# Long convolution with a routed expert step: spreading the loads over each pass, folding in the joint part in single steps, and giving every second set of folds to VectorE

## The chip, the cores and the metric

The kernel runs on one core of a Trainium2 chip. The metric is the device time of one execution in microseconds (us). The engines are TensorE (PE in the profile; its weight loads are PEld), VectorE (DVE), ScalarE (ACT), GpSimd (POOL) and SyncE (SP), which here only issues DMA transfers. Each engine works through its own instructions in the order in which they were written. SyncE does the same with its transfers: a transfer whose condition isn't met yet holds up those written after it.

## The reference

`x` has 8 batches of 6336 positions and 128 features, `h` is a filter of 6336 positions for each feature. The first part is a causal convolution along the positions, by FFT. The second part scores every position of a batch, takes the 128 best, puts them through a two-layer expert and adds the gated result.

```python
L = 2 * S
Xf = np.fft.rfft(x, n=L, axis=1)
Hf = np.fft.rfft(h, n=L, axis=0)
y = np.fft.irfft(Xf * Hf[None], n=L, axis=1)[:, :S, :]
...
scores = np.einsum('bsd,d->bs', y, w_gate)
for b in range(B):
    top_idx = np.argpartition(-scores[b], 128)[:128]
    xe = y[b, top_idx]
    ye = np.maximum(xe @ w1, 0.0) @ w2
    g = 1.0 / (1.0 + np.exp(-scores[b, top_idx]))
    out[b, top_idx] = xe + g[:, None] * ye
```

## The kernel before

The transform is done as matrix products. The work is cut into 8 **passes** (`i` from 0 to 7), each for two batches and half of the features. A pass's data comes in 8 **blocks** `g` of 512 KB (`load_x`, L142). Global block numbers run on: 0 to 7 are the filter, 8 to 15 pass 0, 16 to 23 pass 1, and so on; the text counts a block within its set of 8.

These steps turn up in the profile under their lines:

- `fold` makes of a block its difference and its sum, two elementwise operations of 128 x 512 (L155 into `odd`, which lies in `two` or in `slots`; L156 in place). Both are on GpSimd, except at the start.
- `stage_a` multiplies the folded block with `fa` on TensorE (L169); ScalarE copies the result to `ys` (L183).
- `stage_b` works on 13 **chunks** of 8 wavenumbers. TensorE multiplies with a table that is loaded for each chunk (`load_w`, L197; matmuls at L211), VectorE multiplies with the filter's spectrum (`load_h`, L203; four operations at L220), GpSimd combines (L231). When a chunk is done, the table and the spectrum of the third chunk on are loaded.
- `weigh` adds one of 64 columns of `ys` into the scores, one VectorE operation each (L308).
- `stage_c` multiplies with `wc` (L329), ScalarE copies to `zs` (L335). `stage_d` multiplies with the tables `at` (`load_at`, L348; matmuls at L359), ScalarE copies (L367), and the result is stored (L369).
- A **route** (`scores`, `pick`, `gather`, `expert`) handles the two batches of a pair of passes: scores and the search for the 128 best run on VectorE and TensorE in odd passes, the gathers (L502) and the two experts (L544, L556) in the even pass behind it, or at the end. Its steps are put between the others by `aside`.

All order is written out by hand. The program starts with the filter and pass 0 through `stage_a` (to about 50 us), then comes the **joint part**, `stage_b_first`, where the filter and pass 0 go through stage B together (L265, L281, L284; 13 steps `ci`, to 95 us). Then the passes follow. A pass has 33 **items**: 17 of stage C and 16 of stage D of this pass. Into the items, stages A and B of the *next* pass are put by `plan`: one block of stage A per item in items 0 to 7 (pass 0 takes two at item 0), then two chunks of stage B at each of seven items, which are 8, 10, 12, 14, 16, 17, 19 in even passes and 9, 13, 17, 20, 23, 26, 29 in odd ones. In even passes, the weighing of this pass goes with stage C, and that of the next pass with the items above 19. Odd passes weigh nothing.

Block `g + 2` is folded in the item of block `g`; the first two blocks of the next set are folded at block 7. Blocks have five buffers (`RX`), so block `g + 5` is loaded when stage A of `g` has been through TensorE. Three chunk tables (`RW`) and three of the spectrum (`RH`) are held, and six `at` tiles (`RA`).

At a pass's border the loads stand together: at its end three of the spectrum and six of `at`, at its beginning three tables of 512 KB. The constants of the route and the expert's weights (1 MB) are loaded at item 12 of pass 0. In the joint part, the first six `at` and the first three of the spectrum are loaded from step 7 on, and blocks 0 and 1 of the next set are folded on VectorE in the last two steps.

Of the kernel before, what the change touches and what calls it, by code (L numbers as in the profile page):

```python
# [12 lines left out]
ALU = mybir.AluOpType  # L13
# [7 lines left out]
NU = 8  # L21
# [8 lines left out]
RX, RW, RH, RA = 5, 3, 3, 6  # L30
kchunks = [(k, min(KC, N1 - k)) for k in range(0, N1, KC)]
NC = len(kchunks)
# [3 lines left out]
def conv_moe(ctx, tc, x, h, wg_d, w1, w2, fa_d, wb_d, wc_d, at_d, wgl_d, tri_d, cst_d, tw_d, fb_d, *out):  # L36
# [61 lines left out]
    pos = cp.tile([N1, 2, 2, 66], BF16, name="pos")  # L98
    acc = cp.tile([128, 2, 2, 2, N1], F32, name="acc")

    def load_constants(later):
        if not later:
            sp.dma_start(out=wc, in_=wc_d)
            sp.dma_start(out=wgl, in_=wgl_d)
            return
        sp.dma_start(out=tri, in_=tri_d)
        sp.dma_start(out=cst, in_=cst_d)
        sp.dma_start(out=wg, in_=wg_d.rearrange("(o d) -> o d", o=1).broadcast_to([128, D]))
        sp.dma_start(out=tw, in_=tw_d)
        sp.dma_start(out=fb, in_=fb_d)  # L110
        sp.dma_start(out=w1s, in_=w1)
        sp.dma_start(out=w2s, in_=w2.rearrange("(c p) d -> p c d", p=128))

    def make_constants():
        v.tensor_copy(out=upper16, in_=upper)
# [10 lines left out]
    raw, odd = {}, {}  # L126
# [14 lines left out]
        src = h if i < 0 else x[i]  # L141
        sp.dma_start(out=raw[g], in_=src[:, n].rearrange("p (s d n) -> p s d n", s=2, d=8))  # L142

    def fold(g, eng):
        if g >= 8 * (NU + 1):
            return
        a = raw[g]
        if g < 16:
            o = low(1, 512, g % 7)
        elif g % 8 % 3 < 2:  # L150
            o = two[:, g % 8 % 3]
        else:
            o = low((g // 8 - 1) % 2, 512, 6)
        odd[g] = o.rearrange("p (d n) -> p d n", d=8)
        eng.tensor_tensor(out=odd[g], in0=a[:, 1], in1=a[:, 0], op=ALU.subtract)  # L155
        eng.tensor_tensor(out=a[:, 0], in0=a[:, 0], in1=a[:, 1], op=ALU.add)  # L156

    def stage_a(g, r, dve=()):
        a, o = raw.pop(g), odd.pop(g)
# [39 lines left out]
    def load_h(u, ci):  # L199
        if ci < NC:  # L200
            k0, kn = kchunks[ci]
            hts[u, ci] = tp.tile([128, 2, KC, 32], F32, tag="h", name="ht", bufs=RH)
            sp.dma_start(out=hts[u, ci][:, :, 0:kn], in_=hd[:, ci, u, :, 0:kn])  # L203
# [106 lines left out]
    def stage_c(i, weighing=True):  # L310
        r = i % 2
        y = ys[r].rearrange("p (j c) k t -> p j c k t", c=2)
        z = zs[r].rearrange("p (n g j) m t -> p n g j m t", g=2, j=2)
        banks = [None, None]
        n = 0
        for s in range(66):
            while weighing and n < min(64, 8 * s // 5 + 5):
                weigh(i, n)
                n += 1
            cols = [s, s - 2]  # L320
            for g in range(2):
                if 0 <= cols[g] < 64 and cols[g] % 4 == 0:
                    banks[g] = psa()
            for ri in range(2):
                for g in range(2):
                    c = cols[g]
                    if 0 <= c < 64:
                        rows = slice(g * 64, g * 64 + 64)
                        pe.matmul(banks[g][0:N1, c % 4 * 128:c % 4 * 128 + 128], y[rows, c // 2, ri, :, c % 2],  # L329
                                  wc[rows, ri], start=(ri == 0), stop=(ri == 1))  # L330
            on_pe(0.49)
            for g in range(2):
                c = cols[g]
                if 0 <= c < 64 and c % 4 == 3:
                    act.copy(out=z[:, c // 4, g].rearrange("p j m t -> p j t m"),  # L335
                             in_=banks[g][0:N1].rearrange("p (j t m) -> p j t m", j=2, t=2))
            if i == NU - 1 or (i % 2 and s in (46, 62)):
                aside()
            if s % 4 == 3 or s == 65:
                yield  # L340
# [3 lines left out]
    def load_at(n):  # L344
        if n < 17:
            k = min(2, NT - 2 * n)
            ats[n] = tp.tile([N1, 2, 2, N1], F32, tag="at", name="at", bufs=RA)
            sp.dma_start(out=ats[n][:, 0:k], in_=at_d[:, 2 * n:2 * n + k])  # L348
# [254 lines left out]
    with tc.manual_schedule():  # L603
# [16 lines left out]
        for ci in range(NC):  # L620
            stage_b_first(ci)
            if ci == 3:
                load_constants(False)
            if ci in (4, 5, 6, 9, 10):
                load_x(16 + (4, 5, 6, 9, 10).index(ci))
            if ci >= NC - 2:
                fold(18 + ci - NC, v)
            if 7 <= ci:
                load_at(ci - 7)
            if ci >= NC - RH:  # L630
                load_h(1, ci - NC + RH)

        for i in range(NU):
            phase[0] = i
            if i < NU - 1:
                for ci in range(RW):
                    load_w((i + 1) % 2, ci)
            cs, ds = stage_c(i, i % 2 == 0), stage_d(i)
            g0 = 16 + 8 * i
            plan = {}  # L640
            if i < NU - 1:
                for n in range(8):
                    plan.setdefault(max(0, n - (i == 0)), []).append(("a", n))
                for n, at_item in enumerate((8, 10, 12, 14, 16, 17, 19) if i % 2 == 0 else (9, 13, 17, 20, 23, 26, 29)):
                    plan[at_item] = [("b", k) for k in range(2 * n, min(NC, 2 * n + 2))]
            early = 0
            calm[0] = 0.3 if i < NU - 1 else 0.0
            for item in range(33):
                place[0] = item
                strand = cs if item < 17 else ds  # L650
                if i == 0 and item == 12:
                    load_constants(True)
                if i == 0 and item == 20:
                    make_constants()
                if item in plan:
                    aside()
                    for kind, k in plan[item]:
                        if kind == "a":
                            g = g0 + k
                            if g % 8 < 6:  # L660
                                fold(g + 2, pool)
                            elif g % 8 == 7:
                                fold(g + 1, pool)
                            stage_a(g, (i + 1) % 2)
                            load_x(g + RX)
                            if g % 8 == 7:
                                fold(g + 2, pool)
                        else:
                            stage_b(i + 1, k)
                if i % 2 == 0 and item > 19:  # L670
                    for _ in range(5):
                        if early < 64:
                            weigh(i + 1, early)
                            early += 1
                next(strand, None)
            for st in (cs, ds):
                for _ in st:
                    pass
            if i < NU - 2:
                for ci in range(RH):  # L680
                    load_h(i % 2, ci)
            if i < NU - 1:
                for n in range(RA):
                    load_at(n)
        phase[0] = NU
        idle(7)
        for _ in routes:
# [135 lines left out]
```

## Time and profile before

| | |
|---|---|
| time, median of 3 runs | 954.77 us (952.27 to 965.12) |
| the profiled execution | 949.83 us, span 948.1 us |
| TensorE busy | 889.5 us, 94% of the span |
| VectorE busy | 663.7 us, 70% |
| GpSimd busy | 473.1 us, 50% |
| ScalarE busy | 386.0 us, 41% |
| HBM traffic | 135.38 MB read, 32.96 MB written, 178 GB/s over the span |
| mean granted clock of TensorE | 0.968 |

A row of a chain of work gives start, length and what ran: an engine with the line of the kernel, or a transfer. A row of waits says who waited for whom: microseconds in total, times, the longest. In a row of a timeline, the bracket at the end is the idle time of that engine just before. A row of stretches gives for each engine its busy time and, in brackets, its number of instructions, then the granted clock, the DMA share and the rate. A matmul of 32-bit floats shows as two instructions.

### The profile page before, as it was taken

What the parts mean: (1) busy time and instruction counts of PE and PEld (TensorE: products, weight loads), DVE (VectorE), ACT (ScalarE), POOL (GpSimd) and SP (SyncE); (2) the same over time, 40 slices, a digit from 0 to 9 for tenths busy, and PEclk for the clock granted to TensorE, in tenths of its full rate; (3) what the DMA queues carried; (4) which work ended last, traced back from release to release, by engine and by line L of the source; (5) the groups of instructions that cost most, each with busy time, mean ns of one, the idle gap of its engine ahead of it and who ended that gap; (6) DMA issues with size and microseconds to landing.
All of it is one profiled execution on the core that took longest, in us unless ns stands there. A gap on an engine that the chain in (4) does not pass through costs nothing.

```text
span 948.1 us, 37606 instructions
## 1 busy us (share of the span) xinstructions
PE 889.5 (94%) x16548; PEld 793.2 (84%) x16548; DVE 663.7 (70%) x1488; ACT 386.0 (41%) x612; POOL 473.1 (50%) x376
## 2 busy tenths in 40 slices
PE   5799898999999699999999969999999989999996
PEld 5799797889987689878988769978998779978875
DVE  6467996776688937784788928793779847696631
ACT  4523552248412543237421633236621543234531
POOL 0068875526455686526554586714646475630002
PEclk8899799999999989999999989999999979999999
DMA  9557757467474746457465836457456614543051
GB/s 358 205 194 269 245 156 240 148 185 260 142 238 142 265 138 181 133 160 266 136 218 181 275 97 195 149 154 272 139 166 236 211 59 156 163 146 108 7 179 35
DMA packets 74096, 170.79 MB, mean 180 GB/s; under 512 B 10478, under 2 KB 26828, under 8 KB 73932
## 3 DMA queue, kind: packets, MB, share of 16 engines
q1 hardware_dynamic: 72908, 167.33, 54.0%
q8 instruction: 130, 2.13, 0.9%
q0 software_dynamic: 1024, 1.05, 0.5%
q14 instruction: 34, 0.28, 0.1%
HBM read 135.38 MB, written 32.96 MB: 178 GB/s over the span
## 4 chain that ended last, share of the span: by engine, by line
PE 85%; DMA 5%; POOL 5%; DVE 2%; issue 2%; SPq 0%; ACT 0%; POOLq 0%; ACTq 0%; DVEq 0%
PE pa L359 24%; PE pa L329 24%; PE pb L211 17%; PE pb L169 10%; PE pb L265 3%; DMA xr<-in_x 3%; POOL slots L155 3%; PE pa L265 2%; PE m L544 1%; PE m L556 1%; PE pa L169 1%; POOL xr L156 1%; DMA slots<-tab_wb 1%; PE m L381 1%; DVE acc L308 1%
## 5 line engine op out<-in xcount | busy, mean ns | idle before, releaser
L231 POOL TENSOR_TENSOR slots<-slots,tx 128x512 f32<-128x512 f32 (+1 forms) x182 | 231.2, 1301 | 161.3 <-DVE tx L220 161.2
L329 PE MATMUL pa<-wc,slots 64*99 64x128 f32 x4096 | 268.2, 279 | 2.9 <-issue 2.9
L329 PEld LDWEIGHTS pa<-wc,slots 64*99 64x99 f32 x4096 | 243.9, 170 | 16.5 <-issue 4.8
L335 ACT COPY slots<-pa 99x512 f32<-99x512 f32 x256 | 163.5, 639 | 193.2 <-PE pa L329 185.9
L359 PE MATMUL pa<-slots,at 99*99 99x256 f32 (+1 forms) x1056 | 232.9, 374 | 0.7 <-ACT slots L335 0.7
L308 DVE SCALAR_TENSOR_TENSOR acc<-slots,wgl,acc 128x198 f32<-128x198 f32 x496 | 208.0, 493 | 2.6 <-POOL slots L231 2.6
L359 PEld LDWEIGHTS pa<-slots,at 99*99 99x99 f32 x1056 | 164.4, 163 | 51.8 <-ACT slots L335 0.9
L220 DVE TENSOR_TENSOR slots<-pb,ht 128x512 f32<-128x512 f32 (+1 forms) x182 | 119.5, 657 | 105.6 <-issue 59.4
L211 PEld LDWEIGHTS pb<-slots 128*64 128x64 f32 x5544 | 169.3, 137 | 13.3 <-issue 8.4
L211 PE MATMUL pb<-slots 128*64 128x64 f32 x5544 | 176.5, 223 | 4.0 <-DMA slots<-tab_wb 3.7
L367 ACT COPY yt<-pa 99x512 f32<-99x512 f32 x128 | 75.0, 586 | 225.1 <-PE pa L359 219.7
L183 ACT COPY slots<-pb 128x792 f32<-128x792 f32 x130 | 110.7, 901 | 72.9 <-PE pb L169 72.7
L169 PE MATMUL pb<-fa,xr 50*64 50x99 f32 x1840 | 99.7, 258 | 21.9 <-POOL xr L156 18.8
L220 DVE TENSOR_TENSOR tx<-pb,ht 128x512 f32<-128x512 f32 (+1 forms) x182 | 118.8, 653 | 0.0
L169 PEld LDWEIGHTS pb<-fa,xr 50*64 50x64 f32 x1840 | 87.1, 140 | 34.7 <-POOL xr L156 19.5
L155 POOL TENSOR_TENSOR slots<-xr 128x512 f32<-128x512 f32 x13 | 36.6, 2812 | 106.4 <-PE pa L359 56.7
L169 PE MATMUL pb<-fa,two 50*64 50x99 f32 x1344 | 71.1, 255 | 4.4 <-issue 4.4
L156 POOL TENSOR_TENSOR xr<-xr 128x512 f32<-128x512 f32 x53 | 72.7, 1372 | 4.2
L284 POOL TENSOR_TENSOR slots<-slots,tx 128x256 f32<-128x256 f32 (+1 forms) x50 | 37.9, 782 | 61.5 <-DVE tx L281 59.9
L155 POOL TENSOR_TENSOR two<-xr 128x512 f32<-128x512 f32 x40 | 60.8, 1520 | 10.9 <-PE pb L169 10.5
L502 POOL DMA_INDIRECT xe<-out,iu x16 | 15.6, 978 | 100.3 <-DMA out<-yt 88.3
L169 PE MATMUL pb<-fa,slots 50*64 50x99 f32 x1040 | 51.4, 290 | 12.1 <-DVE slots L156 6.7
(151 smaller groups left out, 702.1 us busy)
## 6 DMA issues: line engine op xcount, KB each, us to landing
slots<-tab_wb SPq DMA_DIRECT2D x86, 512.0 KB
xr<-in_x SPq DMA_DIRECT2D x59, 512.0 KB
out<-yt SPq DMA_DIRECT2D x128, 198.0 KB
ht<-hd SPq DMA_DIRECT2D x84, 256.0 KB
at<-tab_at SPq DMA_DIRECT2D x128, 153.1 KB
hd<-slots SPq DMA_DIRECT2D x12, 512.0 KB
slots<-in_h SPq DMA_DIRECT2D x8, 512.0 KB
xr<-tab_wb SPq DMA_DIRECT2D x8, 512.0 KB
```

The costliest lines, as they stand in the source:

```text
L155: eng.tensor_tensor(out=odd[g], in0=a[:, 1], in1=a[:, 0], op=ALU.subtract)
L156: eng.tensor_tensor(out=a[:, 0], in0=a[:, 0], in1=a[:, 1], op=ALU.add)
L169: pe.matmul(bank[c * 64:c * 64 + 64, d * N1:(d + 1) * N1], src, fa[rows, c], start=True, stop=True)
L183: act.copy(out=to, in_=src)
L211: pe.matmul(banks[c][g * 64:g * 64 + 64, j * 64:j * 64 + 64], wt[:, j, c * 64:c * 64 + 64], y[:, g, :, k0 + j], start=True, stop=True)
L220: v.tensor_tensor(out=dst, in0=banks[c][:, 0:kn * 64].rearrange("p (k b j t) -> p k b j t", k=kn, b=2, t=2), in1=ht[t].rearrange("p k (j t ...
L231: pool.tensor_tensor(out=d3, in0=d3, in1=tx.rearrange("p k (j t) -> p k j t", t=2), op=ALU.add if c else ALU.subtract)
L308: v.scalar_tensor_tensor(out=dst, in0=col, scalar=w, in1=dst, op0=ALU.mult, op1=ALU.add)
L329: pe.matmul(banks[g][0:N1, c % 4 * 128:c % 4 * 128 + 128], y[rows, c // 2, ri, :, c % 2], wc[rows, ri], start=(ri == 0), stop=(ri == 1))
L335: act.copy(out=z[:, c // 4, g].rearrange("p j m t -> p j t m"), in_=banks[g][0:N1].rearrange("p (j t m) -> p j t m", j=2, t=2))
L359: pe.matmul(pt[0:N1, o:o + w * 128], ats[tau // 2][:, tau % 2, c], z[:, c, q:q + w], start=(c == 0), stop=(c == 1))
L367: act.copy(out=yt.rearrange("p b q d -> p q b d"), in_=pt[0:N1].rearrange("p (q b d) -> p q b d", q=4, b=2))
```

## The change

1. `load_constants` has three parts. `wc` and `wgl` stay in the joint part; the route's five small constants come at item 16 of pass 0 instead of item 12 (what is made of them at item 24 instead of 20); the expert's two weights come at item 20 of pass 1.
2. The three tables and three spectra of the next pass are loaded one by one in items 1 to 6 of each pass, in turn, and the six `at` in items 9 to 14 (2 to 7 in the last pass). They leave the joint part, the pass's beginning and its end.
3. Blocks 0 and 1 of the set behind the joint part are folded in steps 8 to 11 of it, one of the four operations per step, still on VectorE.
4. In even passes the folds of blocks 2 to 7 are on VectorE instead of GpSimd. Blocks 0 and 1, and all of the odd passes, stay on GpSimd.
5. Weighings of stage C are spread more thinly: five per item instead of six or seven.

```diff
-    def load_constants(later):
-        if not later:
+    def load_constants(part):
+        if part == 0:
             sp.dma_start(out=wc, in_=wc_d)
             sp.dma_start(out=wgl, in_=wgl_d)
+        if part == 2:
+            sp.dma_start(out=w1s, in_=w1)
+            sp.dma_start(out=w2s, in_=w2.rearrange("(c p) d -> p c d", p=128))
+        if part != 1:
             return
...
-    def fold(g, eng):
+    def fold(g, eng, part=0):
...
-        eng.tensor_tensor(out=odd[g], in0=a[:, 1], in1=a[:, 0], op=ALU.subtract)
-        eng.tensor_tensor(out=a[:, 0], in0=a[:, 0], in1=a[:, 1], op=ALU.add)
+        if part < 2:
+            eng.tensor_tensor(out=odd[g], in0=a[:, 1], in1=a[:, 0], op=ALU.subtract)
+        if part != 1:
+            eng.tensor_tensor(out=a[:, 0], in0=a[:, 0], in1=a[:, 1], op=ALU.add)
...
-            while weighing and n < min(64, 8 * s // 5 + 5):
+            while weighing and n < min(64, 5 * s // 4 + 5):
...
             if ci in (4, 5, 6, 9, 10):
                 load_x(16 + (4, 5, 6, 9, 10).index(ci))
-            if ci >= NC - 2:
-                fold(18 + ci - NC, v)
-            if 7 <= ci:
-                load_at(ci - 7)
-            if ci >= NC - RH:
-                load_h(1, ci - NC + RH)
+            if 8 <= ci < 12:
+                fold(12 + ci // 2, v, 1 + ci % 2)
 
         for i in range(NU):
             phase[0] = i
-            if i < NU - 1:
-                for ci in range(RW):
-                    load_w((i + 1) % 2, ci)
...
+            at_first = 9 if i < NU - 1 else 2
...
-                if i == 0 and item == 12:
-                    load_constants(True)
-                if i == 0 and item == 20:
+                if i == 0 and item == 16:
+                    load_constants(1)
+                if i == 0 and item == 24:
                     make_constants()
+                if i == 1 and item == 20:
+                    load_constants(2)
+                if i < NU - 1 and 1 <= item < 7:
+                    (load_h if item % 2 == 0 else load_w)((i + 1) % 2, (item - 1) // 2)
+                if 0 <= item - at_first < RA:
+                    load_at(item - at_first)
...
                             if g % 8 < 6:
-                                fold(g + 2, pool)
+                                fold(g + 2, pool if i % 2 else v)
...
-            if i < NU - 2:
-                for ci in range(RH):
-                    load_h(i % 2, ci)
-            if i < NU - 1:
-                for n in range(RA):
-                    load_at(n)
```

More of the change, by code (lines that the diff above doesn't have):

```diff
@@ L110, in load_constants @@
         sp.dma_start(out=fb, in_=fb_d)
-        sp.dma_start(out=w1s, in_=w1)
-        sp.dma_start(out=w2s, in_=w2.rearrange("(c p) d -> p c d", p=128))
     def make_constants():
@@ L622, in conv_moe @@
             if ci == 3:
-                load_constants(False)
+                load_constants(0)
             if ci in (4, 5, 6, 9, 10):
                 load_x(16 + (4, 5, 6, 9, 10).index(ci))
-            if ci >= NC - 2:
-                fold(18 + ci - NC, v)
-            if 7 <= ci:
-                load_at(ci - 7)
-            if ci >= NC - RH:
-                load_h(1, ci - NC + RH)
+            if 8 <= ci < 12:
+                fold(12 + ci // 2, v, 1 + ci % 2)
         for i in range(NU):
             phase[0] = i
-            if i < NU - 1:
-                for ci in range(RW):
-                    load_w((i + 1) % 2, ci)
             cs, ds = stage_c(i, i % 2 == 0), stage_d(i)
```

## The prediction

> **What bounds the kernel now.** I read the page's head, then the table of TensorE's waits, then the busy time by pass, then the chain around each gap, then the queues that the chain names.
>
> ```profile
> span 948.1 us, 37606 instructions
> PE 889.5 (94%) x16548; PEld 793.2 (84%) x16548; DVE 663.7 (70%) x1488; ACT 386.0 (41%) x612; POOL 473.1 (50%) x376
> PE pb L169 <- POOL xr L156: 18.8, 3, 7.7
> ```
>
> TensorE is busy for 94% and no other engine is near it, so time can only come from TensorE's gaps and from what follows them. The third line is its longest wait: three times it stood for a fold on GpSimd (L156 is the fold's addition). Busy time by stretch, in the order PE, PEld, DVE, ACT, POOL, granted clock, DMA share and GB/s, puts these in passes. The stretches are the joint part, then passes 0, 1, 2, 4 and 6:
>
> ```profile
> 50.00:95.00 45.00, 45.00 (x774) 44.75 (x770) 33.75 (x95) 15.34 (x32) 34.34 (x46) 0.99 0.73 245
> 95.00:205.60 110.60, 103.56 (x1951) 92.10 (x1951) 94.81 (x201) 43.62 (x64) 65.11 (x46) 0.94 0.60 193
> 205.60:306.90 101.30, 101.18 (x1993) 88.91 (x1995) 71.41 (x160) 43.32 (x64) 56.53 (x43) 1.00 0.61 198
> 306.90:423.00 116.10, 106.84 (x2016) 95.47 (x2017) 86.51 (x188) 46.65 (x76) 66.57 (x50) 0.97 0.55 175
> ...
> 524.00:642.00 118.00, 108.93 (x2027) 96.81 (x2027) 87.86 (x194) 47.06 (x78) 68.62 (x51) 0.97 0.55 174
> 743.00:862.00 119.00, 112.62 (x2023) 100.16 (x2022) 87.72 (x194) 46.82 (x77) 63.52 (x46) 0.94 0.47 150
> ```
>
> Pass 1 takes 101 us with hardly a gap and the clock at 1.00. Passes 2, 4 and 6 take 116 to 119, pass 0 takes 110.6. What should they take? The blocks of the chain at full clock give it:
>
> ```profile
> 339.19 1.52 PE pb L169 x60
> 340.71 1.93 PE pa L329 x32
> 346.09 3.92 PE pb L211 x128
> 284.57 4.43 PE pa L359 x20
> ...
> 934.26 2.68 PE pa L544 x24
> 939.62 1.80 PE pa L556 x16
> ```
>
> A pass holds 8 blocks of L169 (12.2 us), 16 of L329 (30.9), 99 x 8 matmuls of L211 (24.3) and 33 x 4 of L359 (29.2): 96.6 us. Two experts take 934.26 to 941.42, 7.2 us, and passes 2, 4 and 6 hold two each: 104 us. So pass 0 loses 14.0 us, the other even passes 12 to 15 each.
>
> The chain of pass 2, and SyncE's queue ahead of it:
>
> ```profile
> 316.45 9.27 DMA xr<-in_x
> 325.85 6.62 POOL slots L155
> 333.86 2.92 PE pb L169 x64
> ...
> 564.57 3.92 PE pb L211 x128
> ...
> 784.85 3.93 PE pb L211 x118
> ```
> ```profile
> 308.29 1.29 SPq L203 DMA_DIRECT2D ht<-hd  x3
> ...
> 313.91 2.43 SPq L197 DMA_DIRECT2D slots<-tab_wb  x3
> 316.45 28.18 SPq L142 DMA_DIRECT2D xr<-in_x  x8
> ```
> ```profile
> 324.00:326.00 2.00, 0.72 (x12) 0.73 (x14) 2.00 (x8) 0.00 (x0) 0.15 (x1) 1.00 1.02 414
> ```
>
> Stage A's first block ended near 308.4 (306.9 + 1.52) and freed the buffer of block 5, but its load was issued only at 316.45: twelve loads stood ahead, three of the spectrum, six of `at` (the line left out) and three tables, 3.2 MB by the sizes in the code, 8 us at the 414 GB/s of a full stretch. It landed 9.27 us later. Then the fold, on GpSimd, lasted 6.62 us. With L169 and L329 alternating, an item lasts 3.45 us; eight items from 306.9 end at 334.5, but the first L211 stands at 346.09. Loss: 11.6 us, of which 1.4 is the slow block after the gap (2.92 against 1.52). The same reckoning from 524.0 and 743.0 to the first L211 of passes 4 and 6 (564.57, 784.85) gives 13.0 and 14.3. Sum 38.9 us.
>
> Pass 0 loses at two places. At the joint part's end:
>
> ```profile
> 97.65 0.27 PE L169 MATMUL pb<-fa,xr 50*64 50x99 f32 x1 [2.65 <-issue]
> 96.41 1.14 DVE L156 TENSOR_TENSOR xr<-xr 128x512 f32<-128x512 f32 x1
> 98.27 0.34 DVE L281 TENSOR_TENSOR tx<-pb,slots 128x192 f32<-128x192 f32 x1
> 103.44 3.66 PE pa L329 x24
> 107.10 2.47 PE pb L169 x64
> 100.00:104.00 4.00, 3.82 (x77) 3.31 (x71) 4.00 (x4) 2.25 (x3) 3.92 (x3) 0.50 1.05 376
> ```
>
> The row calls the 2.65 us "issue", but L169 starts as the fold's L156 ends (97.55). The fold also holds back the last multiplications, which free the PSUM pair for the block's second half. Two blocks of L169 should take 3.04 us from 95.0; L329 begins at 103.44, so 5.4 us are lost, and at clock 0.50 the next blocks lose (3.66 - 1.45) + (2.47 - 1.52) = 3.2 more. Later the constants:
>
> ```profile
> PE pb L211 <- DMA slots<-tab_wb: 3.7, 1, 3.7
> 152.27 0.43 SPq L112 DMA_DIRECT2D w2s<-in_w  x1
> 152.80 7.18 DMA slots<-tab_wb
> 160.11 3.59 PE pb L211 x64
> ```
>
> Seven loads of constants, 1.5 MB, went ahead of a table that TensorE was waiting for; the last of them is the first SyncE row here. That is 3.7 us of gap and 3.59 - 1.96 = 1.6 us of slow block, 5.3.
>
> **The change part by part.** Prices of VectorE first. Rows: weighings with GpSimd held out (325.8 to 331.4), weighings beside folds on GpSimd (308.2 to 315.8), ten weighings in passes 2 and 0 beside L231, a fold operation on VectorE alone (min/median/max), one step of L220.
>
> ```profile
> L308 DVE SCALAR_TENSOR_TENSOR acc<-slots,wgl,acc 128x198 f32<-128x198 f32 x17 | 5.8, 411 | 0.0
> L308 DVE SCALAR_TENSOR_TENSOR acc<-slots,wgl,acc 128x198 f32<-128x198 f32 x7 | 9.8, 1468 | 0.0
> 353.02 4.98 DVE L308 SCALAR_TENSOR_TENSOR acc<-slots,wgl,acc 128x198 f32<-128x198 f32 x10
> 137.57 6.09 DVE L308 SCALAR_TENSOR_TENSOR acc<-slots,wgl,acc 128x198 f32<-128x198 f32 x10
> L155 DVE TENSOR_TENSOR slots<-slots x11: 683/687/694, 5.2 to 29.5; 128x512 f32<-128x512 f32 x11
> 144.26 0.60 DVE tx L220
> ```
>
> A weighing costs 0.34 us alone, 1.4 beside GpSimd's folds, 0.50 to 0.61 beside L231. While VectorE ran its weighings without a break, GpSimd's fold lasted until they ended: that is the 6.62.
>
> The Trainium skill (SBUF - State Buffer, "SBUF: two separate sides") calls the port pair of VectorE and GpSimd an exclusive lock, held for one instruction, with the other engine fully blocked. The rows agree on blocking, and go further: 17 instructions passed while GpSimd waited. By this rule the single folds in the joint part meet L284 there; the terms below stay as they are.
>
> *Loads.* Tables (L197), spectrum (L203) and `at` (L348) leave the pass's border: one load per item, w at items 1, 3, 5, h at 2, 4, 6, `at` at 9 to 14. Block 5 is then next in the queue when stage A frees its buffer (308.4), with only output stores ahead. An item asks for at most 1 MB, 3.45 us x 414 GB/s carries 1.4 MB, so it lands 2 to 4 us after issue. VectorE reaches its fold at item 3, 9 us after. Each moved load has cover: the first table is due at item 8, seven items (24 us) after its issue, the last (item 5) at item 10; the first `at` at item 17, past 24 us of L211 behind item 9. Where cover goes, TensorE stands for one landing, 7.18 us above. SyncE waits in order: behind each block's load, which waits for TensorE's block, stands the next table; the item pace keeps that harmless.
>
> *Folds.* In an even pass six pairs go to VectorE: 12 x 0.6 to 0.69 us, 8 us, in items 0 to 5. With weighings at 5 per item (after 8 in item 0) an item asks 1.3 + 1.7 = 3.0 us of VectorE against TensorE's 3.45, and GpSimd holds only gathers there. So VectorE keeps ahead, the 1.4 us price falls away, and the 38.9 us go. The first two folds of each set stay on GpSimd, and odd passes keep theirs.
>
> *Weighings.* What is late next: 21 instead of 10 weighings remain when L211 begins (T), five per item for four items. VectorE then does two chunks by T + 2.1 + 4.8 = 6.9, ten weighings (w), two chunks (4.8), ten more, one chunk (2.4): 14.1 + 2w. TensorE's chunk 6 needs that PSUM pair at T + 23.4. w = 4.98 gives a stall of 0.7, w = 6.09 one of 2.9; with 0.4 for the next chunk I take 1.1 in passes 2, 4, 6 (the row of that place) and 2.0 in pass 0. The ends: 0 (the experts' matmuls delay TensorE too) and 18.7 (all at 1.4 us).
>
> *Single folds in the joint part.* Four operations move ahead of the end; VectorE and GpSimd are idle for 11 us of those 45 each. Bounds: 0, and 5.5 us (each 0.69 long, and as long a wait for GpSimd's L284); I take 0.5, nearest to the slack. The last of them still stands ahead of the last multiplications: these end near 97.9, not 98.6. Block 16's first half starts at 95.1 without a wait, its second at 97.9 (2.0 us of gap), L329 at 100.2. Left: 2.0, and half of the 3.2 us of slow clock (1.6), as the gap is shorter than the one that brought it.
>
> The Trainium skill (TensorE: Matmul & The Clock Gate, "What's actually happening") lowers the clock after an idle window of some 3.4 us. Here the clock reached 0.50 behind a gap of 2.65. By that rule the 2.0 us gap would cost no clock and the sum be 1.6 lower; by the row, up to 1.6 higher.
>
> *Constants.* Five small loads at item 16, the two weights (1 MB) in pass 1: the 5.3 us go. First readers are the scores in pass 1 and the experts in pass 2, a pass later. The end of the program is untouched.
>
> **Sum.** Pass 0: 5.4 + 3.2 + 5.3 = 13.9, less 2.0 + 1.6 + 2.0, is 8.3. Passes 2, 4, 6: 38.9 - 3.3 = 35.6. Joint part -0.5. Together 43.4 from the profiled execution's 949.83 (span 948.1): 906. The median of the runs shown, 954.77, stands 0.5% above that execution; so 910 is what I give.
>
> **Rivals.**
> 1. *VectorE becomes the bound behind T.* For: even passes already hold 87 us of it, and the weighings move toward L231. Against: the 4.98 was taken at that place. At 0.8 us per weighing the stall is 6.7 + 0.4, four times 28 in place of 5.3: 929, or 934 on the median's scale. 0.14.
> 2. *Block loads stay late*, because bandwidth and not order held them. Against: 3.2 MB stood ahead. Only pass 0 gains: 942, or 946. 0.08.
> 3. *Slower.* A late block now stops VectorE, which is in order, with the weighings and multiplications behind the fold; before, it stopped GpSimd alone. If block 5 lands over 9 us after its issue, the 38.9 stay and some 9.3 us per even pass come on top: 950 + 37 - 8 = 979, or 984. 0.05.
> 4. *The new order changes nothing*, other loads delaying as much: 955. 0.03.
>
> The forecast holds 0.70, with 899 to 921 as its own range (no stall left at one end, 2.9 us and the single folds' upper bound at the other). The range for 8 in 10 reaches through rival 1: 897 to 936. About 2% is what a measurement of this kernel can tell. Faster by over 2% (below 936): 0.70 plus most of rival 1 and a little of 2, 0.85; within 2%: 0.10; slower: 0.05.
>
> **What would show it.** Right: no wait of L169 for a fold in even passes, passes 2, 4, 6 near 105 us with clock 1.00, block 5 issued at the pass's second block, no 7 us landing in pass 0, L329 near 100. Wrong: VectorE rows of L155 beginning late behind `xr<-in_x`; waits of L211 for L220 behind item 12; ten weighings over 6 us; a wait of L359 for `at`.

## The result and the profile after

The changed kernel takes 909.03 us in the median (907.28 to 913.52, 5 runs) against 954.19 us (952.27 to 965.12, 5 runs) for the one before. The ratio is 0.9515, with a 95% interval of 0.9455 to 0.9576. The profiled execution of the changed kernel took 913.52 us, the longest of its five, with a span of 911.7; the one of before, 949.83 us, was shorter than all of that kernel's timed runs. So the two traces are 36.4 us of span apart, and the medians 45.2. The change adds lines to the file, so the line numbers move: L142 becomes L144, L155 L158, and from the fold's L156 (now L160) on all move by four: L169 is L173, L211 L215, L220 L224, L308 L312, L329 L333, L502 L506.

The head of the page after:

```profile
span 911.7 us, 37567 instructions
...
PE 879.4 (96%) x16548; PEld 783.6 (86%) x16548; DVE 666.7 (73%) x1536; ACT 386.4 (42%) x612; POOL 385.6 (42%) x328
```

TensorE lost only 10 us of busy time (slow blocks), the other 26 us were gaps. GpSimd gave up 48 operations and 87.5 us; VectorE took them over and got only 3 us busier. TensorE's waits after:

```profile
PE pb L173 <- issue: 7.9, 7, 3.8
PE pb L173 <- DVE slots L160: 6.7, 1, 6.7
PE pb L215 <- DVE tx L224: 2.0, 5, 0.8
PE pb L215 <- DMA slots<-tab_wb: 1.2, 3, 0.5
PE pb L173 <- ACT slots L187: 1.0, 1, 1.0
PE pb L173 <- DVE tx L285: 0.5, 1, 0.5
```

The 18.8 us for the fold on GpSimd are gone, and so is the one wait of 3.7 us for a table; three short ones, 1.2 us in all, are left. The 6.7 us are at the start of the program, as before. The stretches of the joint part, pass 0, 1, 2, 4 and 6, in the same columns as before:

```profile
51.00:96.40 45.40, 45.40 (x780) 45.22 (x780) 35.22 (x96) 15.24 (x32) 35.18 (x46) 0.98 0.67 229
96.40:200.10 103.70, 100.55 (x1950) 89.09 (x1951) 88.56 (x212) 43.70 (x65) 43.36 (x35) 0.97 0.63 202
200.10:302.20 102.10, 101.43 (x1992) 89.14 (x1994) 71.31 (x158) 43.26 (x64) 54.57 (x43) 1.00 0.64 207
302.20:409.20 107.00, 105.70 (x2016) 94.11 (x2017) 88.94 (x202) 46.64 (x76) 46.98 (x38) 1.00 0.60 190
...
511.15:616.90 105.75, 105.10 (x2016) 93.75 (x2017) 89.00 (x202) 46.63 (x76) 46.96 (x38) 1.00 0.62 192
718.90:826.00 107.10, 106.00 (x2020) 94.16 (x2020) 89.08 (x202) 47.19 (x77) 41.87 (x34) 1.00 0.52 166
```

Passes 2, 4 and 6 now have hardly a gap, at clock 1.00. To place the difference I read where the first matmul of stage A falls in each pass, from stretches of 0.05 us. "Stage A span" here is the time from there to the first matmul of stage B in the pass; without a loss it is 27.6 us (eight times 3.45).

| from first L169 (L173) | before, us | after, us | difference |
|---|---|---|---|
| start to pass 1 | 207.25 | 201.75 | -5.5 |
| pass 2, of it stage A span | 117.85, 39.2 | 108.8, 29.6 | -9.05 |
| pass 4, of it stage A span | 117.95, 39.3 | 107.5, 28.3 | -10.45 |
| pass 6, stage A span alone | 40.6 | 28.9 | -11.7 |
| passes 1, 3, 5 and all behind | | | +0.3 |
| span | 948.1 | 911.7 | -36.4 |

How stage A of pass 2 runs now, on SyncE's queue and on VectorE (the last two rows are the ten weighings, twice, that stand between the chunks of stage B):

```profile
303.82 0.36 SPq L144 DMA_DIRECT2D xr<-in_x  x1
304.23 0.43 SPq L201 DMA_DIRECT2D slots<-tab_wb  x1
```

```profile
312.03 0.68 DVE L158 TENSOR_TENSOR slots<-xr 128x512 f32<-128x512 f32 x1
...
338.62 4.98 DVE L312 SCALAR_TENSOR_TENSOR acc<-slots,wgl,acc 128x198 f32<-128x198 f32 x10
348.32 4.96 DVE L312 SCALAR_TENSOR_TENSOR acc<-slots,wgl,acc 128x198 f32<-128x198 f32 x10
```

Stage A starts at 302.1; its first block frees the buffer 1.52 us later, and block 5 is issued at 303.82, with the first table behind it and not ahead. It is folded at 312.03, in 0.68 us. Before, it was issued 8 us after the buffer was free, and the first operation of its fold ended at 332.5.

### The profile page after: what moved, and what is told of

Read it like the earlier page. It is cut to its first block, busy times and chain, and to the rows that moved or that the text cites. A ratio compares the mean times of both kernels' runs of the same rounds, so it can differ in the third digit from the quotient of the medians.

```text
span 911.7 us, 37567 instructions
## 1 busy us (share of the span) xinstructions
PE 879.4 (96%) x16548; PEld 783.6 (86%) x16548; DVE 666.7 (73%) x1536; ACT 386.4 (42%) x612; POOL 385.6 (42%) x328
## 4 chain that ended last, share of the span: by engine, by line
PE 80%; DVE 12%; issue 3%; DMA 3%; ACT 1%; SPq 0%; POOLq 0%; POOL 0%; ACTq 0%; DVEq 0%
PE pa L363 24%; PE pa L333 23%; PE pb L173 12%; PE pb L215 11%; DVE acc L312 4%; DVE tx L224 4%; DVE slots L224 3%; PE pb L269 3%; DMA slots<-tab_wb 2%; PE m L560 1%; PE pa L269 1%; PE pa L173 1%; PE m L548 1%; PE m L385 1%; DVE slots L285 1%
## 5 line engine op out<-in xcount | busy, mean ns | idle before, releaser
L333 PE MATMUL pa<-wc,slots 64*99 64x128 f32 x4096 | 262.8, 276 | 1.0 <-issue 1.0
L333 PEld LDWEIGHTS pa<-wc,slots 64*99 64x99 f32 x4096 | 239.3, 167 | 13.5 <-issue 1.8
L312 DVE SCALAR_TENSOR_TENSOR acc<-slots,wgl,acc 128x198 f32<-128x198 f32 x496 | 184.5, 443 | 3.4 <-POOL slots L235 3.4
L215 PEld LDWEIGHTS pb<-slots 128*64 128x64 f32 x5544 | 168.2, 136 | 13.3 <-issue 4.7
L215 PE MATMUL pb<-slots 128*64 128x64 f32 x5544 | 175.9, 222 | 3.3 <-DVE tx L224 2.0
L224 DVE TENSOR_TENSOR slots<-pb,ht 128x512 f32<-128x512 f32 (+1 forms) x182 | 119.3, 656 | 65.7 <-issue 39.8
L187 ACT COPY slots<-pb 128x792 f32<-128x792 f32 x130 | 110.8, 901 | 44.7 <-PE pb L173 44.4
L224 DVE TENSOR_TENSOR tx<-pb,ht 128x512 f32<-128x512 f32 (+1 forms) x182 | 118.6, 652 | 0.0
L173 PE MATMUL pb<-fa,xr 50*64 50x99 f32 x1840 | 94.5, 249 | 2.5 <-issue 1.5
L173 PEld LDWEIGHTS pb<-fa,xr 50*64 50x64 f32 x1840 | 81.8, 133 | 11.3 <-issue 4.1
L173 PE MATMUL pb<-fa,two 50*64 50x99 f32 x1344 | 68.9, 249 | 0.0
L158 POOL TENSOR_TENSOR two<-xr 128x512 f32<-128x512 f32 x24 | 31.5, 1313 | 82.6 <-PE pb L173 61.6
L288 POOL TENSOR_TENSOR slots<-slots,tx 128x256 f32<-128x256 f32 (+1 forms) x50 | 39.3, 809 | 61.1 <-DVE tx L285 60.0
L506 POOL DMA_INDIRECT xe<-out,iu x16 | 18.9, 1179 | 105.4 <-DMA at<-tab_at 71.0
L173 PE MATMUL pb<-fa,slots 50*64 50x99 f32 x1040 | 48.9, 285 | 13.2 <-DVE slots L160 6.7
L173 PEld LDWEIGHTS pb<-fa,two 50*64 50x64 f32 x1344 | 59.3, 133 | 0.2 <-issue 0.2
L173 PEld LDWEIGHTS pb<-fa,slots 50*64 50x64 f32 x1040 | 43.5, 161 | 13.2 <-DVE slots L160 6.7
```

Source lines behind the costliest of these rows:

```text
L173: pe.matmul(bank[c * 64:c * 64 + 64, d * N1:(d + 1) * N1], src, fa[rows, c], start=True, stop=True)
L187: act.copy(out=to, in_=src)
L215: pe.matmul(banks[c][g * 64:g * 64 + 64, j * 64:j * 64 + 64], wt[:, j, c * 64:c * 64 + 64], y[:, g, :, k0 + j], start=True, stop=True)
L224: v.tensor_tensor(out=dst, in0=banks[c][:, 0:kn * 64].rearrange("p (k b j t) -> p k b j t", k=kn, b=2, t=2), in1=ht[t].rearrange("p k (j t ...
L288: pool.tensor_tensor(out=d3, in0=d3, in1=tx[:, c, 0:w].rearrange("p k (j t) -> p k j t", t=2), op=ALU.add if c else ALU.subtract)
L312: v.scalar_tensor_tensor(out=dst, in0=col, scalar=w, in1=dst, op0=ALU.mult, op1=ALU.add)
```

## The experiments

They ran in three groups, each with the kernel before and the changed kernel itself on the same chip. The changed kernel is the yardstick of each: e1, e5 and f1.

> The changed kernel once more, to have a second profile of it beside the kernels of this call. Its first profiled execution (913.5 us) was the slowest of five, their median 909.0. Theory 1 (the extra is the start-up's own scatter, and clock after its gaps): near 909 us, passes 2, 4 and 6 again 106 to 107 us, pass 0 again 103 to 104, the stretch up to the joint part's end between 95 and 96.4. Theory 2 (the passes themselves scatter): the passes differ by more than 1 us from the first profile.

> The changed kernel as the yardstick of this call. It gave 909.0 us first and 922.2 the second time, where TensorE's waits named issue were 12 and 20 us. If those waits make the difference, a time near 909 goes with some 12 us of them and one near 922 with some 20.

> The changed kernel as the yardstick of this call. Earlier profiles of it showed three waits of some 0.35 us named issue in the first two blocks of passes 2, 4 and 6 (31 us from a pass's first block to its first L215) or none there (29 us). Expected: 909 to 922 us, with 29 us where those waits are missing and 31 us where they stand.

Against the kernel before they gave 0.9619 (0.9581 to 0.9658, median 922.23 us), 0.9579 (0.9531 to 0.9627, 919.67 us) and 0.9593 (0.9549 to 0.9638, 921.39 us). The kernel before took 956.84, 957.91 and 958.74 beside them. So the gain is there each time, but 35 to 38 us rather than 45. Neither expectation of e1 on the time held: it isn't near 909 us, and its passes differ from the first profile by more than the 1 us of Theory 2 (pass 2 takes 112.3 us in place of 108.8). The waits that the view calls "issue" sum up on TensorE to 11.8 us in the result's trace, 19.3 in e1, 15.9 in e5 and 19.0 in f1. They go with the time, but not in the proportion that e5 asked for: with 15.9 us of them it took 919.67. f1 came out as expected, 921.39 us with some 31 us of stage A where the short waits stand.

In the table, stage A is the sum of the three spans of passes 2, 4 and 6, and "rest" is pass 2 behind it (78.6 before).

| run | what differs | median us | ratio (95%) | stage A, us | rest, us |
|---|---|---|---|---|---|
| before | | 954.19 | 1 | 119.1 | 78.6 |
| result | the change | 909.03 | 0.9515 (0.9455 to 0.9576) | 86.8 | 79.2 |
| e1 | the change | 922.23 | 0.9619 (0.9581 to 0.9658) | 93.2 | 80.8 |
| e2 | folds on GpSimd | 915.63 | 0.9554 (0.9520 to 0.9587) | 86.5 | 81.8 |
| e3 | folds and pace alone | 936.81 | 0.9782 (0.9745 to 0.9820) | 96.1 | 81.3 |
| e4 | constants at once | 927.81 | 0.9683 (0.9642 to 0.9724) | 93.2 | 80.8 |
| e5 | the change | 919.67 | 0.9579 (0.9531 to 0.9627) | 91.4 | 80.8 |
| e6 | joint folds as before | 925.90 | 0.9652 (0.9601 to 0.9703) | 97.8 | 80.8 |
| e7 | weighings ahead of T | 915.33 | 0.9536 (0.9488 to 0.9584) | 91.6 | 80.2 |
| e8 | folds on GpSimd, old pace | 924.77 | 0.9627 (0.9576 to 0.9677) | 86.0 | 85.4 |
| f1 | the change | 921.39 | 0.9593 (0.9549 to 0.9638) | 94.1 | 80.8 |
| f2 | folds on GpSimd | 917.39 | 0.9555 (0.9515 to 0.9596) | 86.9 | 81.9 |
| f3 | gathers later | 912.20 | 0.9496 (0.9455 to 0.9538) | 85.9 | 80.0 |
| f4 | tables at the border | 920.31 | 0.9585 (0.9545 to 0.9625) | 91.1 | 80.8 |

### The loads without the folds (e2, f2)

```diff
-                                fold(g + 2, pool if i % 2 else v)
+                                fold(g + 2, pool)
```

> The changed kernel, but all folds of the even passes on GpSimd as before; loads, constants, single folds and weighing pace as changed. Theory A (order of the loads and port lock each hold the block back): the block arrives in time, but GpSimd, once idle, is locked out by some 35 weighings at 0.34 us, so block 5 is folded near 24 us into the pass where 17 are due: each of passes 2, 4, 6 loses 6 to 8 us against the change, pass 0 some, 930 us. Theory B (the order of the loads alone was the cause): 910 us. Theory C (the fold's engine alone was the cause): passes 2, 4, 6 as before the change, 945 us.

> The changed kernel with all folds of even passes on GpSimd, once more. Theory B (the loads carry the gain; VectorE's folds add nothing, and the waits named issue come with them): again below the yardstick, by 3 to 7 us, stage A of passes 2, 4, 6 at 28 to 30 us. Rival (both kernels are the same and the 6.6 us were scatter): within 2 us of it.

With the folds of blocks 2 to 7 back on GpSimd, and everything else as changed, the kernel is not slower but faster: by 6.6 us in the first group, by 4.0 in the third. The intervals of the two ratios overlap, hardly in the first group and by half in the third, so the sign is fairly sure and the size is not. Stage A takes 86.5 and 86.9 us, close to the 82.8 without a loss. GpSimd and VectorE of e2 in pass 2:

```profile
311.25 1.40 POOL L158 TENSOR_TENSOR slots<-xr 128x512 f32<-128x512 f32 x1
...
318.92 1.28 POOL L158 TENSOR_TENSOR two<-xr 128x512 f32<-128x512 f32 x1
...
324.26 6.53 POOL L158 TENSOR_TENSOR two<-xr 128x512 f32<-128x512 f32 x1 [2.68 <-PE pb L173]
```

```profile
301.02 25.14 DVE L312 SCALAR_TENSOR_TENSOR acc<-slots,wgl,acc 128x198 f32<-128x198 f32 x30
...
326.55 3.10 DVE L312 SCALAR_TENSOR_TENSOR acc<-slots,wgl,acc 128x198 f32<-128x198 f32 x9
```

GpSimd's folds take 1.3 to 1.4 us each while VectorE is weighing; it is VectorE that is held, to 25.14 / 30 = 0.84 us a weighing, and it has the time. Only behind a pause of 2.68 us is a fold shut out, for 6.53 us: it ends at 330.79, 1.1 us after VectorE's last weighing (329.65). That one is for the next set. It fits the 6.62 us before: there the late block had left GpSimd without work for 8.95 us, VectorE was running without a break when it landed, and the fold ended 1.1 us after the weighings (332.47 and 331.34). With the loads in the new order, the folds need not move for the gain of the even passes.

### The folds without the loads (e3)

```diff
# in the kernel before, its line numbers
-                                fold(g + 2, pool)
+                                fold(g + 2, pool if i % 2 else v)
...
-            while weighing and n < min(64, 8 * s // 5 + 5):
+            while weighing and n < min(64, 5 * s // 4 + 5):
```

> The kernel before, with only two edits: the folds of blocks 2 to 7 of even passes on VectorE, and five weighings per item. Loads and constants stand at the border as before. Theory A: block 5 still lands near 18 us into the pass, VectorE stops for it with the weighings behind, but folds it at once; each of passes 2, 4, 6 loses 3 to 6 us against the change in place of 11, and the joint end and constants their 5 + 5: 930 us. Theory B (loads alone): 953 us. Rival 3 of the prediction (a late block stops VectorE and comes on top): above 965 us.

936.81 us, 20 us under the kernel before in its group, where the change is 35 under it. In stage A it takes off 23.0 us (119.1 to 96.1), and the change in the same group 25.9 (to 93.2). The chain, and VectorE, of pass 2:

```profile
318.39 8.40 DMA xr<-in_x
```

```profile
326.88 0.69 DVE L155 TENSOR_TENSOR slots<-xr 128x512 f32<-128x512 f32 x1 [6.78 <-DMA xr<-in_x]
```

The block is still issued late and lands 8.40 us after. VectorE stands 6.78 us for it (5.78 and 7.21 in passes 4 and 6), with the weighings behind it, and then folds at once. The fold is done at 328.3, and TensorE comes to this block at 330.1, so it does not wait; in passes 4 and 6 it comes 3.3 and 2.6 us after the fold. A late block without a lock-out thus costs stage A nothing by itself, where the slower rival charged 9.3 us a pass on top of the old loss. The 4.4 us a pass that are left to 82.8 ((96.1 - 82.8) / 3) are waits called "issue" and slow matmuls beside them; e1, whose blocks come early, has 3.5 us of these (the section on f3 has more).

So the old loss took both, a late block and a lock-out behind it, and either set of edits ends it, the loads of e2 or the folds and pace of e3. How much of e3 is the pace is not shown. By an estimate from rows already seen, the thinner pace alone would shorten the lock-out: before, VectorE's last run at that place was 20 weighings (6.79 us), with the thinner pace 9 (3.10 us in e2), so the fold on GpSimd would end up to 3.7 us a pass earlier, 11 of the 36 us. That kernel was not run.

The larger part of e3's distance to e1 lies where e3 is the kernel before: behind the joint part and at the constants (pass 1 begins at 209.2 us against 200.9, and the rest of pass 0 takes 76.8 us against 73.0).

### The constants at once (e4)

```diff
-                if i == 0 and item == 16:
-                    load_constants(1)
-                if i == 0 and item == 24:
+                if i == 0 and item == 12:
+                    load_constants(1)
+                    load_constants(2)
+                if i == 0 and item == 20:
                     make_constants()
-                if i == 1 and item == 20:
-                    load_constants(2)
```

> The changed kernel, but all constants and both weights loaded at item 12 of pass 0 as before (what is made of them at item 20). By the prediction's step: 5.3 us more, 914 us, with a wait of 3 to 4 us of stage B for a table in pass 0 and a slow block behind it. Rival: in the changed order stage B of pass 0 waits for VectorE's weighings at that place anyway, and the wait for the table hides behind that: under 2 us more, 910 us.

5.6 us slower than e1. TensorE's wait for a table is back, and the chain shows the slow block behind it:

```profile
PE pb L215 <- DMA slots<-tab_wb: 3.2, 1, 3.2
```

```profile
151.31 7.10 DMA slots<-tab_wb
158.54 3.56 PE pb L215 x64
```

3.2 + (3.56 - 1.96) = 4.8 us at this place. Not all of it is net: behind its stage A, pass 0 took 76.6 us against 73.0 in e1, 3.6 more. Another 1.4 us lie in pass 0's stage A and 1.3 in pass 1's, which the edit does not touch; in the first of them e1 happened to keep its clock at 1.00 where e4 shows 0.59. The intervals of e1 and e4 touch, too. So the constants are worth some 4 us, between 3.6 and 5.6.

### The joint part's folds whole (e6)

```diff
-            if 8 <= ci < 12:
-                fold(12 + ci // 2, v, 1 + ci % 2)
+            if ci >= NC - 2:
+                fold(18 + ci - NC, v)
```

> The changed kernel, but blocks 0 and 1 folded whole in the last two steps of the joint part, as before. By the prediction's step: stage C begins 3.2 us later behind the joint part's end and the slow clock is as likely or likelier: 3 to 5 us more than the yardstick. Rival: the single folds cost in the joint part what they give at its end: within 1 us.

6.2 us slower than e5 in the median (every execution of e6, 923.59 to 932.03, is above every one of e5, 916.56 to 919.98), 12.2 in the span of the profiled execution. The chains at the joint part's end, of e5 and of e6, and a stretch of e6:

```profile
100.73 3.66 PE pa L333 x24
104.39 2.19 PE pb L173 x61
```

```profile
105.18 3.66 PE pa L333 x24
108.84 2.85 PE pb L173 x64
```

```profile
104.00:108.00 4.00, 4.00 (x52) 3.76 (x46) 3.93 (x12) 1.70 (x2) 0.00 (x0) 0.50 0.48 188
```

L333 starts 4.5 us later, and the block behind it takes 0.7 us longer, with the clock at 0.50. But 1.6 of the 4.5 us arose before that: the joint part's last L269 ended at 96.7 in e6 and at 95.1 in e5, and over all traces, with either way of folding, its end scatters from 94.2 to 97.1. From its last L269 to the first L333 it is 8.4 us in e6, as in the kernel before and in e3, and 4.8 to 5.8 us in the ten traces with single folds in steps 8 to 11. So the single folds are worth about 3 us, 3.5 with the slower block. Another 6.4 us of the profiled execution were lost in stage A, 2.26 of them in one wait of pass 2; this edit does not touch that, and the medians hold less of it.

### The weighings ahead (e7)

```diff
-            while weighing and n < min(64, 5 * s // 4 + 5):
+            while weighing and n < (3 * s // 2 + 5 if s < 24 else min(64, 39 + 13 * (s - 23) // 4)):
```

> The changed kernel, but the weighings of an even pass are all written ahead of item 8: six per item in items 0 to 5, 13 in item 6, the rest in item 7. By the formula 14.1 + 2w the waits of stage B for VectorE (2 us in all, with 1 to 2 us more in pass 0) go, and GpSimd's folds for the next pass are locked out for some 5 us, which nobody waits for: 2 to 4 us less than the yardstick. Rival: the locked-out GpSimd is late with the first combinations of stage B, and the gain is given back: within 1 us, or slower.

4.3 us faster than e5; the intervals of the ratios overlap, so the size is unsure. The traces agree with it: from its first to its last matmul, stage B is 2.3 us shorter in pass 0 (44.7 against 46.9) and 0.6, 0.6 and 0.9 in passes 2, 4 and 6, 4.4 in all. TensorE waits for L224 no more, and GpSimd shows where the lock goes:

```profile
322.73 5.90 POOL L158 TENSOR_TENSOR two<-xr 128x512 f32<-128x512 f32 x1 [17.44 <-PE pb L173]
```

The fold of the next set's first block is shut out for 5.90 us, and nobody needs it for another pass.

### The folds on GpSimd with the old pace (e8)

```diff
-                                fold(g + 2, pool if i % 2 else v)
+                                fold(g + 2, pool)
...
-            while weighing and n < min(64, 5 * s // 4 + 5):
+            while weighing and n < min(64, 8 * s // 5 + 5):
...
-            if 8 <= ci < 12:
-                fold(12 + ci // 2, v, 1 + ci % 2)
+            if 7 <= ci < 11:
+                fold(16 + (ci - 7) // 2, v, 1 + (ci - 7) % 2)
```

> The loads, constants and single folds as changed (the single folds one step earlier, steps 7 to 10), but the folds of even passes on GpSimd and the weighing pace as before the change. In the last call the loads alone were 6.6 us faster than the whole change, as GpSimd's folds stood back to back and VectorE had no block to wait for. Theory B (loads alone carry the gain, the moved folds cost): the old pace takes away the waits of stage B for VectorE as well (3 us in the loads-alone profile), and the earlier single folds bring stage C forward by 0.9 us: 8 to 10 us less than the yardstick. Rival (the 6.6 us were the spread of the instruction waits): within 3 us of it.

The expectation was missed: 924.77 us, 5.1 slower than e5, and not 8 to 10 faster. The run has a third edit, the single folds one step earlier; it did not help either, as the first L333 came 6.3 us after the joint part's last L269, against 5.6 in e5. Stage A is as good as in e2 (86.0), but the rest of the pass grew to 85.4 us:

```profile
PE pb L215 <- DVE tx L224: 8.4, 6, 2.3
```

```profile
326.33 6.80 DVE L312 SCALAR_TENSOR_TENSOR acc<-slots,wgl,acc 128x198 f32<-128x198 f32 x20
```

```profile
323.98 10.29 POOL L158 TENSOR_TENSOR two<-xr 128x512 f32<-128x512 f32 x1 [2.62 <-PE pb L173]
```

With folds on GpSimd a weighing takes VectorE longer (30 in 25.14 us here too), and the old pace puts 20 more behind these where e2 has 9. VectorE runs on without a break to 333.13, GpSimd's fold is shut out for 10.29 us and ends 1.1 us later, and both come late to stage B; the waits for L224 are 8.4 us where e2 has 3.1. So the thinner pace, which looked like a side edit, is what lets the loads work without the folds.

### The gathers later (f3)

Why should the folds on VectorE cost anything? In e1 and f1 the longer stage A has waits that the chain calls "issue". Here is the chain of f1 at the start of pass 2, and GpSimd at that place (first and last of four gathers):

```profile
300.65 1.33 PE pb L173 x50
301.98 0.35 issue
302.34 0.40 PE pb L173 x4
302.74 0.33 issue
303.07 0.50 PE pb L173 x6
```

```profile
300.24 1.10 POOL L506 DMA_INDIRECT xe<-out,iu  x1 [5.05 <-DVE iu L496]
...
306.30 1.09 POOL L506 DMA_INDIRECT xe<-out,iu  x1 [0.30 <-issue]
```

A block of 1.52 us takes 2.9, and the second one 2.6, at a clock of 1.00: waits of some 0.35 us, and between them a few matmuls that follow each other slowly (the ten of the last rows take 0.90 us). Relieved of the folds, GpSimd runs the four gathers within 7 us, from 300.2 to 307.4, which is where these two blocks lie; in e2, with folds between them, they reached from 300.9 to 318.9. f3 holds them back to item 10:

```diff
-            while u and (phase[0] < 2 * p + 2 or (b0 + 2 < B and place[0] < 4)):
+            while (u or b0 + 2 < B) and (phase[0] < 2 * p + 2 or (b0 + 2 < B and place[0] < 10)):
```

> The changed kernel, but the gathers of a pair of passes wait for item 10 of the even pass; before they ran in its first 7 us, all four in a row, as GpSimd had no folds between them. Theory G (the gathers' many small transfers hold up what TensorE's issue waits for): the waits of the first two blocks go, stage A of passes 2, 4, 6 takes 29 us, 4 to 6 us less than the yardstick unless the experts come late. Rival (the waits have another cause): they stay, and the time is within 2 us or longer.

912.20 us, 9.2 less than f1, where 4 to 6 were expected. The two intervals do not meet, and the ratio, 0.9496, is the lowest of all. Stage A falls from 94.1 to 85.9 us. The chain of f3 at the same place:

```profile
299.60 1.52 PE pb L173 x59
...
303.05 1.52 PE pb L173 x61
```

Moving the gathers took these waits away. In the traces they go together: e1, e4, e5, e6, e7, f1 and f4, with four gathers in a row at the pass's beginning, have three such waits, of 0.2 to 0.4 us, in the first two blocks of each of passes 2, 4 and 6; e2, f2 and e8, with folds between the gathers, have one in pass 2 and none in the other two, and f3 has none. How a gather holds TensorE's issue is not shown: the DMA share at that place in f1 was 0.44, far from full. Nor does it happen each time: in the result's trace the gathers stand at the same place (301.76 to 308.9), and the first two blocks take 1.52 us each:

```profile
302.16 1.52 PE pb L173 x59
...
305.61 1.52 PE pb L173 x59
```

f3 also answers the question above: the folds on VectorE cost nothing of themselves. With the gathers held back this kernel is 5.2 us faster than f2, whose folds are on GpSimd (909.45 to 913.99 us against 916.04 to 919.19), with stage A alike (85.9 and 86.9 us) and a shorter rest of the pass (80.0 and 81.9). Folds on GpSimd with late gathers were not run.

### The tables at the border, spectrum in the items (f4)

```diff
-                if i < NU - 1 and 1 <= item < 7:
-                    (load_h if item % 2 == 0 else load_w)((i + 1) % 2, (item - 1) // 2)
+                if i < NU - 1 and item == 0:
+                    for ci in range(RW):
+                        load_w((i + 1) % 2, ci)
+                if i < NU - 1 and item in (2, 4, 6):
+                    load_h((i + 1) % 2, (item - 1) // 2)
```

> The changed kernel, but the three tables of the next pass (1.5 MB) are loaded together at item 0, ahead of the loads of blocks 5 to 7; the spectrum and the other tiles stay spread. Theory (a late block costs only from the point where VectorE's fold needs it, some 9 us after its buffer is free): 2 MB at 414 GB/s and 2 us put block 5 some 7 us after that, just in time, and the time is within 2 us of the yardstick. Rival (any load ahead of the blocks costs): 3 to 4 us per even pass, 10 to 13 us more.

920.31 against 921.39 us for f1: no difference. The queue and the fold of block 5:

```profile
299.45 1.31 SPq L201 DMA_DIRECT2D slots<-tab_wb  x3
301.10 4.85 SPq L144 DMA_DIRECT2D xr<-in_x  x2
```

```profile
309.50 0.69 DVE L158 TENSOR_TENSOR slots<-xr 128x512 f32<-128x512 f32 x1 [0.91 <-DMA xr<-in_x]
```

1.5 MB ahead of the block make VectorE wait 0.91 us for it, and TensorE not at all. So it is not the order as such that counts but the amount: the fold needs its block 9 us after the buffer came free, and behind the 3.2 MB of e3 VectorE waited 5.8 to 7.2 us.

## Why the prediction was right, and where its terms were off

**The place of the loss.** Passes 2, 4 and 6 gained 31.2 of the 36.4 us between the traces, all of it in stage A (32.4 there, 1.2 given back behind it), with clock 1.00, no wait for a fold and block 5 issued at the second block, as forecast. Pass 0 with what is ahead of it gave 5.5.

**The credit to two edits.** The step "Folds: VectorE keeps ahead, the 1.4 us price falls away, and the 38.9 us go" counted the loss once for loads and folds together. That left open which one carries it, and the runs settle it: either does. With the new loads GpSimd's folds come in time (e2, f2: 32.6 us off stage A in e2); with the folds and pace alone TensorE never waits for the late block (e3: 23.0 us off, beside 25.9 in e1, the difference to e2 being mostly the short waits and slow matmuls that e1 has, too). So the folds did not have to leave GpSimd to escape the 6.62 us: that lock-out needed the late block, behind which GpSimd had stood idle. The Trainium skill (SBUF - State Buffer, "SBUF: two separate sides") describes the lock as lasting one instruction; the 6.53, 5.90 and 10.29 us here, each over a run of VectorE's instructions and ending 1.1 us behind it, go further, as the 6.62 us did.

**Mis-sized terms.** The forecast on the profiled execution's scale was 43.4 us, the spans differ by 36.4.
- The 38.9 us were reckoned from the stretch edges 524.0 and 743.0, but the first L169 of passes 4 and 6 stood at 525.2 and 744.1. By first matmuls the loss was 119.1 - 82.8 = 36.3, so 2.6 too much was on the account.
- Stage A came to 86.8 and not 82.8 us: 4.0 us of short waits and slightly slow blocks had no price (2.1 us are waits over 0.2 us that the chain calls "issue"). In the other runs of the same kernel they were 8.6 to 11.3, and f3 puts 8.2 us of f1's 11.3 on the four gathers in a row. The prediction said of GpSimd's new free time only that it "holds only gathers there".
- The stall behind T was priced somewhat too high. w was 4.98 and 4.96, as taken. TensorE's waits for L224 are 2.0 us in all where 5.3 were set, and passes 2 and 4 lost 0.6 each behind stage A; e7, which takes the stall away, shortens stage B by 4.4 us in all.
- The joint part's end won 3.0 us (8.4 to 5.5 from the last L269 to L333), near the 3.4 set, and e6 agrees with 2.8. Half of the slow clock was to go and did not:

```profile
101.86 3.66 PE pa L333 x24
105.52 2.35 PE pb L173 x63
```

```profile
100.00:104.00 4.00, 4.00 (x74) 3.76 (x63) 3.93 (x9) 1.91 (x3) 0.83 (x1) 0.55 0.96 309
```

- The constants were about right (5.3 set, 3.6 to 5.6 in e4), and the rest of pass 0 fell by 4.1 where 3.3 were set. The joint part itself, with the start, grew by 1.4, where 0.5 was set; as its end scatters by 2.9 us over the traces, that term is not measured.

**Why the median is still near.** The forecast of 910 added half a per cent for the median, but the trace of before was that kernel's shortest execution and the trace of after the changed one's longest. The missing 7 us are hidden in that, which is luck. In the three groups the same kernel took 919.67 to 922.23 us: inside the wide range, at the upper end of the forecast's own (899 to 921), and 10 to 12 us above the forecast.

**The rivals.** VectorE as the bound behind T needed 0.8 us per weighing; at 0.50 it did not come, though e8 shows that it was near (8.4 us of waits when VectorE falls behind). Late loads from bandwidth are excluded by f4 and by block 5 itself. The slower rival is excluded by e3: a block that stops VectorE costs TensorE no wait in stage A.

## What to carry to other kernels

In a queue that works in order, put the load whose reader comes first ahead of those that merely fill a buffer, and reckon the bytes ahead of it against the time that its reader can wait: 1.5 MB cost nothing here; 3.2 MB cost 12 us a pass with a reader that was then locked out, and no wait of TensorE in stage A with one that was not. When two edits attack one stall, price each alone: here the new loads were enough, and the second edit, the folds on VectorE, cost 4 to 6.6 us as it stood. And look at what the relieved engine does first with its free time; here it was four gathers in a row, and holding them back took another 9.2 us off and left the folds on VectorE no dearer than on GpSimd.

## What the runs showed of the hardware

- Which of VectorE and GpSimd was held depended here on who had been at work. With GpSimd's folds back to back, or right behind a gather, a weighing took 0.84 us and the fold 1.3 to 1.4. Behind a pause of 2.6 us or more in GpSimd's work, with VectorE running without a break, a fold stood for 5.90 to 10.29 us, and in all six cases looked at (three passes of the kernel before, pass 2 of e2, e7 and e8) it ended 1.1 us after VectorE's last weighing.
- TensorE's issue was held for about 0.35 us at a time while GpSimd ran four gathers in a row (f1), and not when these ran later (f3). The cause is open, and it was not there in the result's trace.
- The clock was 0.55 after the joint part though TensorE's waits there were only 1.0 and 0.5 us. In e1, with the same two waits, it stayed at 1.00, as it did in f4; the other traces with single folds had 0.50 to 0.65 from 100 to 104 us:

```profile
102.00:106.00 4.00, 3.73 (x94) 3.27 (x94) 3.97 (x11) 2.26 (x4) 0.00 (x0) 1.00 0.98 352
```

The Trainium skill (TensorE: Matmul & The Clock Gate, "What's actually happening") asks for an idle window of some 3.4 us; no gap of that length stands there. What decides is not shown.
